# A rank for every operation, exp tile by tile in four units, and filler products in planned pauses

## The chip, the cores and the metric

The kernel runs on one core of one Trainium2 chip. The core has five instruction queues that run beside each other: TensorE (PE, matrix products; PEld is its loading of the stationary operand), VectorE (DVE), ScalarE (ACT), GpSimd (POOL) and SyncE (SP, which here only issues DMAs). Each runs its own list of instructions in order and waits on semaphores for the others. The metric is the device time of one execution in microseconds; the median of several runs counts.

## What is computed

Linear attention with random features for 8 batches of 8 heads (576 tokens, 64 channels, 128 features), and then a feed-forward layer (512 to 2048 to 512 channels, exact GELU) over the 4608 tokens:

```python
q_s, k_s = (q * scale, k * scale)
def phi(x):
    proj = np.einsum('bhsd,md->bhsm', x, omega)
    sq = np.sum(x * x, axis=-1, keepdims=True) / 2.0
    h = proj - sq
    h = h - np.max(h, axis=-1, keepdims=True)
    return np.exp(h) / np.sqrt(m)
q_p, k_p = (phi(q_s), phi(k_s))
kv = np.einsum('bhsm,bhsd->bhmd', k_p, v)
z = np.sum(k_p, axis=2)
num = np.einsum('bhsm,bhmd->bhsd', q_p, kv)
den = np.einsum('bhsm,bhm->bhs', q_p, z)[..., None] + 1e-06
x = (num / den).transpose(0, 2, 1, 3).reshape(4608, 512)
h = x @ w_in
out = (0.5 * h * (1.0 + erf(h / np.sqrt(2)))) @ w_out
```

The term sq is the same for all features of a token, so it falls out when the largest value is taken away.

## The kernel before

**Attention units.** A unit is a pair of heads of one batch; there are 32, four to a batch. Units 0 to 7 ("plain", `unit_plain`) work in float32: `pair` and `shared` project K and Q into PSUM (18 tiles of 128 tokens by 128 features), `top` on DVE takes each row's negative maximum, the exp follows, `kv` is the key-value product, `q_trans` and `q_copy` transpose the Q features, `num_plain` makes numerator and denominator, and `den`, `rcp`, `div` divide into the token buffer `xs`. The exp has two forms. In units 0 to 3 `exp_tiles` reads each tile from PSUM and takes the maximum as its bias, 18 small ACT instructions. In units 4 to 7 `shift_tiles` on DVE adds the maximum and writes to SBUF, and one ACT instruction (`exps`, 2304 columns) does the whole unit. Units 8 to 31 ("split") work with pairs of 16-bit parts: `x_high` and `x_low` split K and Q, `proj` and `proj_q` project them, `exps` is one instruction per unit, `kv_split`, `num` and `back` follow.

**Feed-forward blocks.** There are 18 blocks of 256 tokens. Block 0 runs in float32 (`mm1`, `gelu_plain`, `mm2_plain`). The others use 16-bit parts: `sw1` and `sw2` (function `product`) are the first layer in a seven-product scheme, with `comb_a`, `comb_b`, `comb_c` between them; `gelu`, `g_high` and `g_low` make the two 16-bit parts, and `mm2` is the second layer, into the PSUM buffers "acc". A block has eight chunks.

**Weights.** They come as 64-bit words in 16 pieces of two DMAs each (`w_load`, eight pieces of w_in, then eight of w_out). `w_hi` and `w_lo` (ACT), `w_shift` (DVE) and `w_round` (POOL) turn a piece into float32 in the buffer `w32`; its largest value sets a scale (`wchain_a` to `wchain_f`), and then `a_high`, `a_low`, `s_high`, `s_low` (w_in) and `w_high`, `w_low` (w_out) make the 16-bit parts. `w_high` (line 602) writes `woh`.

**What sets the order.** The program is a graph of operations, each with an engine, a cost in microseconds, and keys that it reads and writes. At build time the class `Planner` steps through a planned time: on each engine, among the operations that are ready and have room in their buffers, the one with the least due time goes next. The result is one fixed list for each engine. The due time comes from tables found outside the program (`STARTS`, `UDUE`, `OFF`, `PO`), propagated backwards through the graph, less a bonus by kind:

```python
p = (o.due - bonus.get(o.kind, 0.0), o.id)
```

PSUM has three buffers "at", three "h" and two "acc". Units of batch 0 may take any of them, units 4 to 7 only "at":

```python
ring = ANY if u.mode == 0 else 'at'
```

`put` writes an operation's instructions and ties them to the one before on the same engine.

Of the kernel before, what the change touches and what calls it, by code (L numbers as in the profile page):

```python
# [41 lines left out]
OFF = dict(a_high=-13.69, a_high2=-2.55, a_low=3.92, a_low2=30.54, back=-0.66, back_c=-53.08, block_be=18.21, block_high=2.46,  # L42
        block_high_1=-26.27, block_low=1.36, block_low_1=-19.02, block_out=1.79, block_scales=-9.32, block_spread=8.72,
        bound_a=-5.8, bound_a_a=-478.94, bound_a_b=1.62, bound_a_c=6.31, bound_b=0.18, bound_b_a=-192.28, bound_b_b=-308.58,
        bound_b_c=14.95, bound_c=-4.72, bound_c_a=85.34, bound_c_b=-108.59, bound_c_c=8.05, chain_a=-1.54, chain_b=3.92,
        chain_c=66.41, chain_d=2.96, comb_a=0.61, comb_a_1=1.25, comb_b=-1.27, comb_b_1=-14.65, comb_c=-0.14, comb_c_1=-8.99,
        den_a=-450.06, den_b=-18.7, div_a=-474.39, div_b=-35.9, exp_tiles_a=88.01, exps=3.6, exps_b=74.83, exps_c=21.55,
        g_high=-0.99, g_high_1=-58.14, g_low=-11.39, g_low_1=2.86, gelu=0.98, gelu_1=3.81, gelu_plain=-27.15, identity=-18.43,
        k_high=-2.66, k_high_c=15.22, k_low=-3.41, k_low_c=-24.51, k_shift=-2.42, k_shift_c=1.96, kv_a=-4935.28, kv_a_c=86.01,
        kv_b=-28.56, kv_b2=-1.97, kv_b2_c=14.8, kv_b_c=17.09, kv_c=7.39, kv_c_c=-27.26, kv_d=2.75, kv_d_c=12.39, kv_split=-2.52,  # L50
        kv_split_c=-3.32, kvz_plain_a=-243.1, kvz_plain_b=5.35, load_dup=-31.91, load_dup_c=179.73, load_om=15.98,
        load_two_a=-43.39, load_two_b=-51.4, load_v_a=-56.35, load_v_b=-128.76, load_vst=52.48, load_vst_c=22.44, mm1=15.82,
        mm2=25.3, mm2_1=0.3, mm2_plain=18.77, norm=-13.96, norm_c=4.14, nothing=1.34, num=-6.46, num_c=15.2, num_plain_a=-13.88,
        num_plain_b=-10.89, p2=2.99, pair_a=-272.72, pair_b=121.03, proj=0.47, proj_add=0.18, proj_add_c=-12.11, proj_c=0.24,
        proj_lo=0.22, proj_lo_c=-23.83, proj_q=0.39, proj_q_c=-12.62, put_x=-2.32, put_x_c=-12.75, q_back=2.77, q_back_c=8.16,
        q_blocks=2.07, q_blocks_c=-41.78, q_copy_a=-396.58, q_copy_b=-6.38, q_high=-0.51, q_high_c=21.5, q_low=0.22,
        q_low_c=-0.57, q_max=2.12, q_max2=0.92, q_max2_c=10.36, q_max3=13.21, q_max3_c=18.46, q_max4=-11.32, q_max4_c=7.99,
        q_max5=0.92, q_max5_c=3.49, q_max6=-15.37, q_max6_c=94.79, q_max_c=-114.63, q_shift=-18.3, q_shift_c=-152.32,
        q_trans_a=513.45, q_trans_b=-13.77, rcp_a=-364.04, rcp_b=29.11, s_high=36.92, s_low=-50.32, s_sum=-467.63,
        scale_om=-24.66, shared_a=-708.55, shared_b=-11.95, shift_tiles_b=7.13, split_om=-36.34, store=-53.19, store_dma=0.58,  # L60
        sw1=0.55, sw1_1=17.68, sw2=0.57, sw2_1=2.01, t_sum=3.22, t_sum_1=-27.4, top_a=-128.4, top_b=-0.8, v_a=4.39, v_a_c=91.42,
        v_b=0.99, v_b_c=-16.74, v_max=-14.06, v_max_c=47.43, v_scales=4.0, v_spread=32.29, vb_ones=-35.4, w_abs_1=-722.49,
        w_hi_0=1.8, w_hi_1=-202.85, w_high=-23.19, w_lo_0=3.69, w_lo_1=-90.29, w_load_0=202.81, w_load_1=4.68, w_low=-134.68,
        w_max_0=5.38, w_max_1=258.53, w_round_0=-55.99, w_round_1=-43.44, w_shift_0=8.21, w_shift_1=6.84, warm=198.7,
        wchain_a=-48.44, wchain_b=43.0, wchain_c=-25.75, wchain_d=7.44, wchain_e=16.02, wchain_f=-27.17, x_high=6.09,
        x_high_c=-14.76, x_low=-3.36, x_low_c=-0.55, zeros=37.43)
# [1452 lines left out]
```

## Time and profile before

| What | us |
|---|---|
| Median of 3 runs (969.47 to 973.82) | 972.83 |
| The profiled execution, its own time | 974.43 |
| Its span, first to last instruction | 972.4 |
| DVE, ACT, POOL busy | 762.8, 736.2, 485.1 |
| First `mm1` of block 0 | 65.15 |
| First second-layer product of block 1 | 154.59 |

In a row of the timeline stand start and length in us, engine, line, operation, what it writes and reads, how many instructions are merged, and in brackets the idle time before it and what ended that. A row of the waits gives the waiting engine and line, the one that it waited for, the sum in us, how often, and the longest. A row of windows gives a stretch, its length, and for each engine its busy time and instructions, then TensorE's granted clock as a share, the busy share of the DMA engines and GB/s. `w` is the name under which the profile shows the buffer `w32`, parts of which serve as a second feature buffer.

### The profile page before, as it was taken

To read this page: it belongs to the slowest core of one execution; us is meant where nothing else is said; L and a number is where in the kernel's file an instruction comes from. 1 tells how busy PE (TensorE), PEld (TensorE's weight loads), DVE (VectorE), ACT (ScalarE), POOL (GpSimd) and SP (SyncE) were. 2 spreads that over 40 slices of the span, in tenths; PEclk is the share of its full clock that TensorE was granted. 3 is DMA by queue.
4 is the path that set the end of the run, shared out by engine and by line. 5 is a ranking of instruction groups with operands and counts; after the bars stand their busy time and mean duration, and the time that the engine had idled before them with its cause. 6 is when DMAs were issued, how large, how long until landed. Compare 5 with 4: busy or idle time off the path is not lost.

```text
span 972.4 us, 25715 instructions
## 1 busy us (share of the span) xinstructions
PE 934.6 (96%) x9956; PEld 692.8 (71%) x9956; DVE 762.8 (78%) x2134; ACT 736.2 (76%) x1573; POOL 485.1 (50%) x717
## 2 busy tenths in 40 slices
PE   7979997889999999899999999999999999999998
PEld 6757655567776777677787777867776777786776
DVE  3878888999987998887987899788888897753432
ACT  5968868688889878877877887888787898653432
POOL 0335663775658545754638564397546764300100
PEclk7979998999999999999999999999999999999999
DMA  8865332223221313121212131212121200000000
GB/s 227 236 187 176 131 92 89 65 85 88 61 64 50 97 43 92 44 74 53 82 40 73 53 96 53 72 40 85 51 72 51 72 26 23 2 24 12 12 23 22
DMA packets 46313, 71.44 MB, mean 73 GB/s; under 512 B 13680, under 2 KB 22256, under 8 KB 46192
## 3 DMA queue, kind: packets, MB, share of 16 engines
q1 hardware_dynamic: 46192, 69.81, 23.9%
q8 instruction: 78, 1.28, 0.5%
q14 instruction: 43, 0.35, 0.1%
HBM read 60.36 MB, written 9.44 MB: 72 GB/s over the span
## 4 chain that ended last, share of the span: by engine, by line
PE 74%; DVE 9%; ACT 5%; POOL 5%; DMA 3%; issue 3%; SPq 1%; POOLq 0%; ACTq 0%; DVEq 0%
PE h L1279 26%; PE acc L1327 9%; PE acc L1328 9%; PE acc L1329 9%; PE h L1266 3%; PE acc L1320 3%; PE at L1007 2%; PE at L1092 2%; PE at L1029 2%; PE at L852 2%; PE at L797 1%; DVE w L1082 1%; DVE gl L1317 1%; DMA vt<-in_v 1%; POOL r L999 1%
## 5 line engine op out<-in xcount | busy, mean ns | idle before, releaser
L999 POOL TENSOR_TENSOR r<-xt,r 64x288 fp32r<-64x288 f32 (+2 forms) x216 | 165.9, 784 | 144.7 <-ACT r L994 83.7
L1279 PE MATMUL h<-xh,w 128*128 128x128 f16 x2176 | 216.2, 219 | 0.0
L1328 PE MATMUL acc<-woh,gl 128*128 128x512 f16 (+1 forms) x544 | 206.0, 379 | 2.5 <-DVE gl L1317 2.5
L1327 PE MATMUL acc<-woh,gh 128*128 128x512 f16 (+1 forms) x544 | 207.0, 381 | 0.9 <-ACT o L1336 0.9
L1329 PE MATMUL acc<-wol,gh 128*128 128x512 f16 (+1 forms) x544 | 205.8, 378 | 0.2 <-DVE wol L605 0.2
L1279 PE MATMUL h<-xl,w 128*128 128x128 f16 x1088 | 198.6, 219 | 0.0
L1279 PEld LDWEIGHTS <-w 128*128 128x128 f16 x3264 | 195.4, 98 | 3.3
L1279 PE MATMUL h<-xh,wih 128*128 128x128 f16 x816 | 157.2, 220 | 8.5 <-DVE gl L1317 4.8
L1279 PE MATMUL h<-xl,wih 128*128 128x128 f16 x816 | 156.5, 219 | 0.0
L1279 PE MATMUL h<-xh,wil 128*128 128x128 f16 x816 | 156.5, 219 | 0.0
L1279 PEld LDWEIGHTS <-wih 128*128 128x128 f16 x1632 | 139.7, 98 | 18.3 <-DVE h L1297 4.1
L1317 DVE SCALAR_TENSOR_TENSOR gl<-h,bs,gh 128x512 f16<-128x512 f32 x136 | 101.0, 744 | 46.2 <-ACT gh L1314 45.7
L1305 ACT ACTIVATE h<-h,bs 128x512 f32<-128x512 f32 x136 | 90.0, 662 | 49.0 <-PE h L1279 42.7
L1314 ACT ACTIVATE gh<-h,bs 128x512 f16<-128x512 f32 x136 | 93.6, 689 | 36.0 <-PE acc L1329 28.9
L1329 PEld LDWEIGHTS <-gh 128*128 128x128 f16 x560 | 55.1, 98 | 63.5 <-issue 1.7
L1279 PEld LDWEIGHTS <-wil 128*128 128x128 f16 x816 | 80.1, 98 | 17.0 <-issue 7.9
L994 ACT CAST r<-xt 128x256 fp32r<-128x256 f32 (+2 forms) x216 | 81.7, 407 | 13.2 <-PE at L1029 7.6
L1328 PEld LDWEIGHTS <-gl 128*128 128x128 f16 x560 | 55.2, 99 | 47.0 <-DVE gl L1317 3.0
L1327 PEld LDWEIGHTS <-gh 128*128 128x128 f16 x560 | 55.0, 98 | 47.2 <-issue 2.1
L1286 ACT COPY g<-h 128x256 f32<-128x256 f32 x136 | 50.4, 370 | 40.8 <-PE h L1279 38.5
L1291 DVE TENSOR_TENSOR g<-h,g 128x128 f32<-128x128 f32 x136 | 38.5, 283 | 39.0 <-ACT g L1286 38.3
L1292 DVE TENSOR_TENSOR h<-h,g 128x256 f32<-128x256 f32 x136 | 58.8, 433 | 4.7
(231 smaller groups left out, 2106.7 us busy)
## 6 DMA issues: line engine op xcount, KB each, us to landing
xt<-in_kT SPq DMA_DIRECT2D x56, 288.0 KB, 3.9
xt<-in_qT SPq DMA_DIRECT2D x56, 288.0 KB, 3.8
out_x<-o SPq DMA_DIRECT2D x35, 256.0 KB, 2.0
raw<-in_w_in SPq DMA_DIRECT2D x16, 512.0 KB, 6.6
raw<-in_w_out SPq DMA_DIRECT2D x16, 512.0 KB, 4.6
...
```

Source lines behind the costliest of these rows:

```text
L994: nc.scalar.copy(G['r', u, x][:, 0:b - a], xf[:, a:b])
L999: nc.gpsimd.tensor_tensor(r, xf[D:, a:b], r, op=ALU.subtract)
L1279: nc.tensor.matmul(h, w[p], x[r], start=first and i + m == 0, stop=last and i == 1 and m == 2, skip_group_check=True)
L1286: nc.scalar.copy(G['sa', n, c], G['h', n, c][:, 0:2 * P])
L1291: nc.vector.tensor_tensor(q, hv[:, 3], sa[:, 0:P], op=ALU.add)
L1292: nc.vector.tensor_tensor(hv[:, 1:3], hv[:, 1:3], q.unsqueeze(1).broadcast_to([P, 2, P]), op=ALU.add)
L1305: nc.scalar.activation(h, h, AF.Gelu, scale=G['bs', n][:, 2:3])
L1314: nc.scalar.activation(G['gh', n, c], G['h', n, c], AF.Copy, scale=G['bs', n][:, 3:4])
L1317: nc.vector.scalar_tensor_tensor(G['gl', n, c], G['h', n, c], G['bs', n][:, 3:4], G['gh', n, c], op0=ALU.mult, op1=ALU.subtract)
L1327: nc.tensor.matmul(acc, gh, woh[:, f, c0:c1], start=f == 0, stop=False)
L1328: nc.tensor.matmul(acc, gl, woh[:, f, c0:c1], start=False, stop=False)
L1329: nc.tensor.matmul(acc, gh, wol[:, f, c0:c1], start=False, stop=f == NF - 1)
```

## The change

**Rank.** The four tables, the backward propagation and the bonus are gone. A table `RANK` with one whole number for each operation is the due time:

```diff
-            o.due = 1e9 if k == 0 else UDUE[n] if k == 2 else add if k == 3 else add + STARTS[n] + (STARTS[n + 1] - STARTS[n] if n + 1 < len(STARTS) else 48.0) * x
-                o.due = min(o.due, s.due - o.c - (lat.get(o.e, 0) + hop.get(s.e, 0) if s.e != o.e else 0))
-            o.due += PO.get(o.id, 0.0)
-            o.due += OFF.get(o.tag, 0.0)
+            o.due = RANK[o.id]
...
-                    p = (o.due - bonus.get(o.kind, 0.0), o.id)
+                    p = o.due
...
+RANK = (0, 0, 0, 0, 1, 5, 2, 3, 8, 1, 2, 49, 4, 7, 2, 3, 5, 9, 16, 17, 13, 11, 3, 17, 38, 30, 4, 11, 13, 14, 2, 12, 19, 13, 20, 23, 25, 21, 23, 36,
```

Some 20 planned costs are changed as well (`den` from 0.5 to 0.35, `num_plain` from 1.0 to 1.15, `a_low` from 0.75 to 0.92, and others), and `proj` and `proj_q` are planned 0.057 us longer where the operation ahead of them on PE carries no mark (`psw`; the projections, `kv_split` and `back` carry one). Planned costs change the order only.

**Exp tile by tile.** The mode of units 4 to 7 becomes that of units 0 to 3, with their PSUM buffers kept to "at":

```diff
-            u.mode = 0 if b == 0 else 1 if u.k < X['plain'] else 2
+            u.mode = 0 if u.k < X['tiles'] else 1 if u.k < X['plain'] else 2
...
-        ring = ANY if u.mode == 0 else 'at'
+        ring = ANY if u.b == 0 else 'at'
```

With X['tiles'] = 8, `shift_tiles` and the whole exp are gone from units 4 to 7; each has 18 exps of one tile.

**Filler products.** Where the planner leaves PE idle by more than 0.9 us ahead of an operation that takes a new PSUM buffer, after 5 us of planned time, `put` writes products of bfloat16 views of the identity into that buffer ahead of the operation's own, whose first product starts over; nothing reads them:

```diff
+            o.idle = t - max(free[o.e], o.free) if o.e == 'PE' else 0.0
...
+        if X['fill'] and o.idle > 0.9 and o.t > 5.0:
+            t = [G[k] for (_, k), name in zip(o.new, o.pick) if name in ANY]
+            for _ in range(int((o.idle - 0.3) * X['fill'] / 0.11) if t else 0):
+                nc.tensor.matmul(t[0][:, 0:256], id16[:, 0:P], id16, start=True, stop=True)
```

The program has 22 of them: 7, 5 and 6 ahead of three of the first four projections, and 4 ahead of a later chunk of the first layer. The number of `ACT_TABLE_LOAD` instructions, which ACT needs between exp and GELU, is 60 in place of 56. `store` also names the block's scales among what it reads; that changes no instruction.

**What moves: the start.** These are the first rows of SP in the program before. `xt` holds K and Q of two units, `om` is omega, `raw` a weight piece, `vt` V.

```order
L750 DMA xt<-in_kT 128x576
L536 DMA om_66<-in_omT 64x128 x2
L750 DMA xt<-in_kT 128x576
L750 DMA xt<-in_qT 128x576 x2
L573 DMA raw<-in_w_in 128x4x256 x4
L746 DMA vt_73<-in_v 128x10x64
L746 DMA vt_74<-in_v 128x10x64
```

And the same place of SP in the changed program, where 545 is the weights' line, 722 that of K and Q:

```order
L508 DMA om_66<-in_omT 64x128 x2
L545 DMA raw<-in_w_in 128x4x256 x2
L722 DMA xt<-in_kT 128x576
L722 DMA xt<-in_qT 128x576
L722 DMA xt<-in_kT 128x576
L722 DMA xt<-in_qT 128x576
L545 DMA raw<-in_w_in 128x4x256 x2
L718 DMA vt_74<-in_v 128x10x64
```

The first weight piece now stands ahead of K and Q; V of the first two units has the same loads ahead of it as before.

**What moves: the exp of unit 4.** These are rows of ACT before, from the last weight maximum (599) to the rows behind the exp (790). Lines 578 and 583 are `w_hi` and `w_lo`, 836 is `q_copy`, 879 `den`, 816 `bound_a`.

```order
L599 ACTIVATE w_71,wmax<-w_71 128x1024
L836 COPY w_71<-h 128x512
L578 ACTIVATE raw<-raw 128x1024
L583 ACTIVATE w_71<-raw 128x1024
L879 ACTIVATE dt<-at 128x288
L790 ACTIVATE et<-et 128x2304
L836 COPY w_71<-acc 128x128
L816 ACTIVATE zr<-w_71 128x2
L578 ACTIVATE raw<-raw 128x1024
```

And rows of ACT at the same place in the changed program; 753 is the exp of tiles, 550 and 555 are `w_hi` and `w_lo`, 808 `q_copy`, 851 `den`, 571 the weight maximum:

```order
L753 ACTIVATE et<-at,nm 128x128 x4
L555 ACTIVATE w_71<-raw 128x1024
L851 ACTIVATE dt<-acc 128x288
L753 ACTIVATE et<-at,nm 128x128 x6
L808 COPY w_71<-h 128x512 x2
L550 ACTIVATE raw<-raw 128x1024
L808 COPY w_71<-at 128x128
L571 ACTIVATE w_71,wmax<-w_71 128x1024
L851 ACTIVATE dt<-acc 128x288
L788 ACTIVATE zr<-kvz 128x2
L555 ACTIVATE w_71<-raw 128x1024
L753 ACTIVATE et<-at,nm 128x128 x4
```

The one exp of unit 4 has become groups of four and six tiles with weight work between them.

**What moves: the split of the output weights.** Rows of ACT before around the twelve splits (602); 1305 and 1314 are `gelu` and `g_high` of block 1, 994 is `x_high`, 1011 `proj_lo`, 633 `s_high`:

```order
L1305 ACTIVATE h<-h,bs 128x512
L1314 ACTIVATE gh<-h,bs 128x512
L602 ACTIVATE woh<-w_71,wsc 128x512 x12
L1011 COPY lo<-at 128x256
L602 ACTIVATE woh<-w_71,wsc 128x512 x2
L633 ACTIVATE w_71<-ts,wsc 128x512
L836 COPY qh<-at 128x512
L994 CAST r<-xt 128x256
L836 COPY qh<-at 128x512
L602 ACTIVATE woh<-w_71,wsc 128x512 x2
```

And in the changed program, where 574 is the split, 605 `s_high`, 1258 `comb_a`, 1277 `gelu`:

```order
L574 ACTIVATE woh<-w_71,wsc 128x512 x9
L753 ACTIVATE et<-at,nm 128x128 x4
L808 COPY qh<-at 128x512
L605 ACTIVATE w_71<-ts,wsc 128x512 x2
L574 ACTIVATE woh<-w_71,wsc 128x512
L753 ACTIVATE et<-at,nm 128x128 x4
L574 ACTIVATE woh<-w_71,wsc 128x512 x2
L808 COPY qh<-at 128x512
L808 COPY qh<-at 128x128
L574 ACTIVATE woh<-w_71,wsc 128x512 x2
L1258 COPY g<-h 128x256
L753 ACTIVATE et<-at,nm 128x128 x2
```

Fourteen of the sixteen splits now stand ahead of the first `gelu` and `g_high` of block 1, with exps and copies between them.

More of the change, by code (lines that the diff above doesn't have):

```diff
@@ L42 @@
[L42 to L66, printed above, removed]
@@ L326, in emit @@
                 c = o.c
-                if o.tab and o.tab != self.tab:
+                if o.e == 'PE':
+                    c += X['psw'] * (o.tab == 'r' and self.ptab is None)
+                    self.ptab = o.tab
+                elif o.tab and o.tab != self.tab:
                     c += X['tsw']
@@ L349, in room @@
         def room(o):
-            t, o.pick, taken = o.ready, [], {}
+            t, o.pick, taken, o.free = o.ready, [], {}, 0.0
             if o.e == 'POOL':
@@ L373, in room @@
                 t = max(t, best[0])
+                o.free = max(o.free, best[0])
                 o.pick.append(best[1])
@@ L455, in favor_attention_ffn @@
     wi32 = w32f[:, 1].rearrange("p c (j w) -> p c j w", j=NJ)
+    id16 = ident.bitcast(BF16)
     ones = cp.tile([1, P], F32, name="ones")
@@ L921, in out_ops @@
         pn = [('pn', u, half, a) for a in range(2)]
-        ring = ANY if u.mode == 0 else 'at'
-        op('PE', 1.0, num_plain, u, half, r=[('qh', u, g) for g in (0, 1, 2)] + [('kvz', u), ('qh', u)] + old, w=keys, new=[(ring, k) for k in pn] + new)
-        op('ACT', 0.5, den, u, half, r=pn, new=[('dt', ('dt', u, half))])
+        ring = ANY if u.b == 0 else 'at'
+        op('PE', 1.15, num_plain, u, half, r=[('qh', u, g) for g in (0, 1, 2)] + [('kvz', u), ('qh', u)] + old, w=keys, new=[(ring, k) for k in pn] + new)
+        op('ACT', 0.35, den, u, half, r=pn, new=[('dt', ('dt', u, half))])
         op('DVE', 1.13, rcp, u, half, r=[('dt', u, half)], new=[('rt', ('rt', u, half)), ('rc', ('rc', u, half))])
@@ L938, in out_split @@
             keys, new, old = places(u, ps)
-            op('PE', 0.11 * n + 0.03, back, u, g, r=[('nx', u), ('nx', u, 0), ('nx', u, 1), 'ident'], new=[(('at', 'h'), ('px', u, g))])
-            op('ACT', sum(0.17 + (c1 - c0) / 1200 for _, c0, c1, _ in ps), put_x, u, g, due=(2, 2 * u.k + g, 0.0, 0.0), r=[('px', u, g)] + old, w=keys, new=new)
+            op('PE', 0.11 * n + 0.01, back, u, g, tab='q', r=[('nx', u), ('nx', u, 0), ('nx', u, 1), 'ident'], new=[(('at', 'h'), ('px', u, g))])
+            op('ACT', sum(0.06 + (c1 - c0) / 1200 for _, c0, c1, _ in ps), put_x, u, g, due=(2, 2 * u.k + g, 0.0, 0.0), r=[('px', u, g)] + old, w=keys, new=new)
     def unit_plain(u):
@@ L1207, in split_post @@
             op('POOL' if X['klp'] else 'DVE', 0.25 + 0.3 * n if X['klp'] else 0.14 + 0.15 * n, k_low, u, g, r=es, w=[('kk', g)])
-        op('PE', 0.77, kv_split, u, r=['vb'] + [('kk', g) for g in range(len(KG))], w=[], new=[('at', pk), ('kvs', ('kvs', u)), ('kvz', ('kvz', u))])
+        op('PE', 0.87, kv_split, u, tab='q', r=['vb'] + [('kk', g) for g in range(len(KG))], w=[], new=[('at', pk), ('kvs', ('kvs', u)), ('kvz', ('kvz', u))])
         op('ACT', 0.22, kv_a, u, r=[pk], w=[('kvs', u)])
@@ L1215, in split_post @@
         for g in range(2):
-            op('DVE', 0.74, q_back, u, g, r=[('eq', u.eb, y) for y in (g, g + 2)], new=[('qt', ('qt', u, g))])
+            op('DVE', 0.71, q_back, u, g, r=[('eq', u.eb, y) for y in (g, g + 2)], new=[('qt', ('qt', u, g))])
             op('ACT', 0.62, q_high, u, g, r=[('qt', u, g)] + ([('qf', u)] if g else []), w=[('qf', u, g)], new=[] if g else [('qf', ('qf', u))])
@@ L1381, in ffn_first @@
                new=[] if p else [('h', hk)], due=(1, n, (c + p * .28) / NS, 0.0), kind='P')
-        op('ACT', 0.16 + 256 / 1200, comb_a, n, c, r=[hk], new=[('g', ('sa', n, c))], kind='F')
+        op('ACT', 0.33, comb_a, n, c, r=[hk], new=[('g', ('sa', n, c))], kind='F')
         op('DVE', 0.65, comb_b, n, c, r=[('sa', n, c)], w=[hk], new=[('g', ('qs', n, c))], kind='F')
@@ L1386, in ffn_first @@
         op('ACT', 0.15 + 512 / 1000, gelu, n, c, r=[('bs', n)], w=[hk], tab='g', kind='F')
-        op('ACT', 0.7, g_high, n, c, r=[('bs', n), hk], new=[('gh', ('gh', n, c))], kind='F')
+        op('ACT', 0.66, g_high, n, c, r=[('bs', n), hk], new=[('gh', ('gh', n, c))], kind='F')
         op('DVE', 0.71, g_low, n, c, r=[('bs', n), hk, ('gh', n, c)], new=[('gl', ('gl', n, c))], kind='F')
@@ L1400, in ffn_second @@
                 if c == nc_ - 1:
-                    op('ACT', 0.68 if n else 0.6, store, n, i, c0, c1, r=[key] + ([('bo', n)] if n >= N32 else []), w=[('o', n, i)] if c0 else [],
+                    op('ACT', 0.68 if n else 0.6, store, n, i, c0, c1, r=[key] + ([('bo', n), ('bs', n)] if n >= N32 else []), w=[('o', n, i)] if c0 else [],
                        new=[] if c0 else [('o', ('o', n, i))], due=(1, n + 1, (lag + i * .6) / nc_, 0.0), kind='F' if n >= N32 else 'F0')
```

43 lines of the change are left out of this document (17 added, 26 removed), and 335 rows, old and new, of tables (PO, RANK, UDUE).

## The prediction

> **What bounds the kernel now.** I read the page first, then the busy time of each engine in five stages, then who waited for whom on TensorE (PE) in them.
>
> ```profile
> span 972.4 us, 25715 instructions
> PE 934.6 (96%) x9956; PEld 692.8 (71%) x9956; DVE 762.8 (78%) x2134; ACT 736.2 (76%) x1573; POOL 485.1 (50%) x717
> PEclk7979998999999999999999999999999999999999
> ```
>
> PE is the bound: 972.4 - 934.6 = 37.8 us are all that a better order can take out of its idle time, and the clock row (a digit for each 24.3 us) is low in the slices from 0, 49 and 146 us. What must be asked is where those 37.8 us stand. The columns of the next view are the stage, its length, and the busy time of PE, PEld, DVE, ACT and POOL.
>
> ```profile
> 0.00:62.00 62.00, 49.42 (x408) 38.90 (x408) 38.92 (x103) 45.24 (x116) 15.66 (x16) 0.84 0.77 224
> 62.00:155.00 93.00, 92.85 (x597) 64.05 (x596) 78.37 (x149) 74.67 (x115) 54.41 (x57) 1.00 0.39 131
> 155.00:210.00 55.00, 43.96 (x376) 28.82 (x375) 50.61 (x139) 43.67 (x99) 32.02 (x57) 0.91 0.25 75
> 210.00:460.00 250.00, 242.01 (x2825) 182.73 (x2824) 218.00 (x653) 204.09 (x453) 150.72 (x230) 0.99 0.24 68
> 460.00:972.40 512.40, 506.34 (x5758) 378.29 (x5757) 376.89 (x1091) 368.51 (x793) 232.32 (x359) 1.00 0.16 47
> ```
>
> PE idles 12.6 us ahead of 62, 0.2 us in 62 to 155, 11.0 us in 155 to 210, 8.0 us in 210 to 460, and 6.1 us in the last 512 us, part of which is the store after the last product. So two short stages hold 23.6 of the 37.8 us, with the low clock (0.84 and 0.91) on top. The waits in these two stages:
>
> ```profile
> PE at L797 <- ACT et L790: 5.4, 1, 5.4
> PE at L797 <- DMA vt<-in_v: 4.9, 1, 4.9
> ...
> PE at L1007 <- ACT qh L836: 2.6, 2, 2.1
> PE at L832 <- ACT qh L836: 2.6, 1, 2.6
> PE at L1092 <- DVE w L1074: 1.9, 1, 1.9
> PE h L1279 <- DVE gl L1317: 1.7, 1, 1.7
> ```
>
> The first two are single pauses: the key-value product (L797) waits for the exp of unit 4, and that of unit 0 for its V. The next two are copies out of PSUM (qh) that ScalarE (ACT) brings late.
>
> **Step 1: the exp of unit 4, tile by tile.** The rows of ACT ahead of that pause, and the product behind it beside the same product at full clock:
>
> ```profile
> 50.38 1.13 ACT L578 ACTIVATE raw<-raw 128x1024 f32<-128x1024 f32 x1 [1.74 <-DMA raw<-in_w_in]
> 51.41 1.12 ACT L583 ACTIVATE w<-raw 128x1024 int32<-128x1024 uint32 x1
> 52.73 2.11 ACT L790 ACTIVATE et<-et 128x2304 f32<-128x2304 f32 x1
> ...
> 24.62 2.26 PE L797 MATMUL at<-vt,w 128*128 128x65 f32 x18
> 54.89 4.22 PE L797 MATMUL at<-vt,et 128*128 128x65 f32 x18 [5.45 <-ACT et L790]
> ```
>
> The one exp of unit 4 stands behind two weight instructions, the first of which waits 1.74 us for its DMA; PE waits 5.45 us and then runs this product 4.22 - 2.26 = 1.96 us slower. In the new order of ACT the 18 tiles of this unit come in groups of four to six, ahead of the weight rows or between them. At most 5.45 + 1.96 = 7.4 us go; what is late next is ACT itself. Its work ahead of the copy that block 0 waits for (the denominator of unit 3, first half) comes to the same in both orders by counts, so only ACT's idle time, 62.0 - 45.2 = 16.8 us, can shrink, and of this the start keeps some (step 2). I take 6 of the 7.4 us; bounds 0 and 7.4.
>
> **Step 2: the start.** One weight piece, two DMAs, goes ahead of the first K.
>
> ```profile
> raw<-in_w_in SPq DMA_DIRECT2D x16, 512.0 KB, 6.6
> 10.00:20.00 10.00, 5.05 (x39) 4.82 (x37) 3.54 (x6) 9.22 (x33) 0.00 (x0) 0.73 1.07 302
> 7.05 1.14 ACT L781 ACTIVATE et<-at,nm 128x128 f32<-128x128 f32 x4 [5.04 <-DVE nm L777]
> 16.51 4.19 PE L797 MATMUL at<-vt,et 128*128 128x65 f32 x18 [4.95 <-DMA vt<-in_v]
> ```
>
> 1.05 MB at 302 GB/s is 3.5 us, by which the first projection, the first exp (7.05 us now) and what follows are late; all of PE's queue stands behind that projection. But V of units 0 and 1 stands behind the same bytes as before (omega, four K and Q, two weight pieces), so the product at 16.51 moves little, and ACT does 2.2 us of weight work in the time. Bounds 0 and +3.5; I take +1.
>
> **Step 3: the products without use.** 22 of them: 18 ahead of the first, third and fourth projections of the start, 4 far behind. Priced by the nearest row, that of the warm-up:
>
> ```profile
> 1.05 4.15 PE L532 MATMUL h<-w 128*128 128x256 bf16 x22 [1.05 <-DVE w L523]
> ```
>
> 4.15 / 22 = 0.19 us each, 3.4 us for the 18. The cover is the wait for the late K and Q of step 2; without it they cost those 3.4 us. None stands ahead of the first key-value product, where the 4.95 us pause and the slow 4.19 us are. So I take 0; bounds -1.9 (that product at full clock) and +3.4.
>
> The Trainium skill's page "TensorE: Matmul & The Clock Gate", section "Part 1: The HAM clock gate", says that the clock stands at half by default, rises after some 3.4 us of steady work, and falls after an idle window of that length. The trace agrees: 4.19 and 4.22 us behind pauses of about 5 us, 2.26 us in steady work. By it the fillers would help only if they left no idle window ahead of that product.
>
> **Step 4: more work for ACT.** One whole exp against 18 tiles, the table loads, and what DVE loses:
>
> ```profile
> 14.15 1.13 ACT L781 ACTIVATE w<-h,nm 128x128 f32<-128x128 f32 x4
> 15.16 1.16 ACT L781 ACTIVATE et<-h,nm 128x128 f32<-128x128 f32 x4
> L790 ACT ACT_TABLE_LOAD x27 | 34.6, 1283 | 0.5
> L786 DVE TENSOR_TENSOR et<-at,nm 128x512 f32<-128x512 f32 (+1 forms) x20 | 11.8, 628 | 0.0
> ```
>
> Four tiles take 1.01 us start to start, 18 take 4.55, so each unit costs ACT 4.55 - 2.11 = 2.4 us more, 9.8 for four. The switches between exp and gelu rise from 56 to 60, 4 x 1.28 = 5.1 us. ACT gains 14.9 us, DVE loses 11.8. In 62 to 155 ACT idles 93.0 - 74.7 = 18.3 us while PE idles 0.2: this hides it. These units may use only the three "at" buffers of PSUM, and a tile now holds one until ACT's exp has read it, not DVE's shift, so a late exp stops PE too. If the cover is gone, it costs up to 14.9 us. The nearest row is that of 62 to 155, so I take 0.
>
> The Trainium skill's page "ScalarE: Activation LUTs", section "What ACT_TABLE_LOAD costs", adds a drain of about 1.38 us to the load, 2.66 us for a switch, which speaks against this change. The measured group differs: 27 loads of 1.283 us with 0.5 us of idle time before all of them. By the page the four switches would be 10.6 us, by the row 5.1.
>
> **Step 5: the late copies at 155 to 210.**
>
> ```profile
> 0.00:149.63 149.63, 114.54 (x223) 0.93 0.56 174
> ...
> 149.63 0.69 ACT L1314 ACTIVATE gh<-h,bs 128x512 f16<-128x512 f32 x1
> 150.21 7.47 ACT L602 ACTIVATE woh<-w,wsc 128x512 f16<-128x512 f32 x12
> 159.68 0.57 ACT L836 COPY qh<-at 128x512 f32<-128x512 f32 x1
> ...
> 154.59 0.38 PE L1327 MATMUL acc<-woh,gh 128*128 128x512 f16 x1
> 160.31 0.33 PE L832 MATMUL at<-ident,et 128*128 128x128 f32 x1 [2.58 <-ACT qh L836]
> ```
>
> ACT splits the output weights in one run of twelve, with the copy of the transposed Q behind it, and PE waits. In the new order 14 of the 16 splits stand ahead of the first g_high, broken up by exps and copies. The waits for qh (5.2 us) and the slow clock behind them should go. What is late next is that first g_high: ACT has ahead of it 64 more tiles (64 x 0.2525 = 16.2 us) instead of four exps (8.4), 14 splits (14 x 0.62 = 8.7), two more loads (2.6), and ten smaller instructions less (about 4): 114.5 + 15.1 = 129.6 us of work. With step 1 taken it must start near 145, so ACT may idle 15 us ahead of it, against 149.6 - 114.5 = 35.1 now. The start keeps about 12 of these. It is tight but can be met, since 18.3 of the 35.1 stand where PE was the bound. I take -5 us; bounds 0 and -11.0.
>
> **Step 6: the rest.** Of the 8.0 us idle in 210 to 460 I take 2 (bounds 0 and 8.0), as DVE, which ends the g_low that PE waits for, has 11.8 us less to do. Behind 460, where PE is full, a new order can only lose: +1 (bounds 0 and +4, the idle time there is 6.1 us now).
>
> **Sum.** -6 + 1 + 0 + 0 - 5 - 2 + 1 = -11 us. The profiled execution took 974.43 us, 2.0 more than its span, and lies 1.6 over the median of 972.83. So 963.4 for such an execution and **962 us** for the median.
>
> **Rivals.** First, **slower: ACT becomes the bound.** For it: 15.1 us more work ahead of the first g_high than now. If ACT keeps its 35.1 us of idle time there, that g_high starts at 164.7 and with it the first second-layer product of block 1; the 14 splits done by then (8.7 us) are given back behind it, net +6.4, 979 us. It decides when ACT idles more than 35.1 - 15.1 = 20 us ahead of it. Against it: the 0.2 us of PE's idle time in 62 to 155.
>
> Second, **no change: the gain waits at the output weights.** The weight conversions stand about as deep in ACT's order as before, so if DMA and their rounding set the pace, PE reaches the second-layer product early and waits until about 154.6; only steps 5 and 6 in small part remain, 970 us. For it: the 1.74 us wait for a weight DMA; against: the queue starts the first piece ahead of K now.
>
> Third, **the fillers do what they are meant for** and the first key-value product runs at full clock: 1.9 us more, 960 us. Against it: none stands ahead of it. If they do nothing, the forecast stands.
>
> Fourth, **much more goes**: steps 1, 5 and 6 to their ends (7.4 + 11.0 + 8.0 - 1), 974.4 - 25.4 - 1.6 = 947 us.
>
> **How the numbers follow.** Chances: forecast (955 to 968) 0.45, third 0.05, fourth (943 to 955) 0.15, no change 0.19, slower 0.16. A difference under 0.5%, 4.9 us, can't be told from none here. Faster: 0.45 + 0.05 + 0.15, less 0.02 for the upper edge of the forecast, 0.63; same 0.20; slower 0.17. The range 946 to 978 leaves out the far half of the fourth and most of the slower one.
>
> **What would show it.** Step 1: no wait of PE over 2 us at the key-value product of unit 4, and the mean clock in 50 to 62 at 0.9 or more. Step 2: the first projection at about 8 us instead of 5. Step 4: ACT busy near 751 us, DVE near 751. Step 5: the first second-layer product (its matmul on woh and gh) at 145 to 151 us, and no wait for qh over 1 us. Step 6: PE idle under 7 us behind 460. A start of that product after 155 us would make the forecast wrong by the slower rival; a wait of PE for the output weights at it, by the second.

## The result, and the profile after

The changed kernel takes 946.70 us (median of four, 945.67 to 947.03), the kernel before 972.64 us in runs beside it. The ratio is 0.9737, with a 95% interval of 0.9712 to 0.9761: 26 us less, where 11 were forecast. The profiled execution took 946.9 us, and its page begins so:

```profile
span 945.1 us, 25838 instructions
PE 926.2 (98%) x9978; PEld 688.2 (73%) x9978; DVE 747.6 (79%) x2114; ACT 747.0 (79%) x1645; POOL 492.2 (52%) x717
PEclk9999999999999999999999999999999999999999
```

PE's idle time fell from 37.8 to 945.1 - 926.2 = 18.9 us, and its busy time by 8.4 us although 22 products were added: the low slices of the clock row are gone. The same five stages as before (stage, length, busy time of PE, PEld, DVE, ACT and POOL with their instructions, granted clock, DMA share, GB/s):

```profile
0.00:62.00 62.00, 54.52 (x462) 40.77 (x464) 40.58 (x110) 51.54 (x140) 18.04 (x18) 0.97 0.84 248
62.00:155.00 93.00, 91.39 (x591) 60.47 (x588) 78.91 (x141) 87.45 (x174) 47.50 (x51) 1.00 0.40 131
155.00:210.00 55.00, 53.62 (x575) 39.88 (x572) 51.54 (x150) 47.46 (x107) 41.91 (x67) 1.00 0.23 71
210.00:460.00 250.00, 245.98 (x2849) 186.02 (x2849) 220.16 (x674) 212.58 (x470) 161.85 (x241) 1.00 0.24 70
460.00:945.10 485.10, 480.73 (x5513) 361.07 (x5511) 356.41 (x1044) 348.00 (x758) 222.92 (x343) 1.00 0.16 46
```

What PE loses in a stage has two parts: its idle time, and what the low clock costs while it works, about (1 - clock) times its busy time. The first stage is cut at 25 us below, by the same view of both kernels: PE was busy 18.20 of 25 us at a clock of 0.80 and 31.22 of 37 us at 0.87, and is now busy 21.44 at 1.00 and 33.09 at 0.95.

| Stage, us | Lost before: idle + clock | Lost after | Change | Forecast |
|---|---|---|---|---|
| 0 to 25 | 6.8 + 3.6 | 3.6 | -6.8 | +1 (steps 2, 3) |
| 25 to 62 | 5.8 + 4.1 | 3.9 + 1.7 | -4.3 | -6 (step 1) |
| 62 to 155 | 0.2 | 1.6 | +1.4 | 0 (step 4) |
| 155 to 210 | 11.0 + 4.0 | 1.4 | -13.6 | -5 (step 5) |
| 210 to 460 | 8.0 + 2.4 | 4.0 | -6.4 | -2 (step 6) |
| 460 to the end | 6.1 | 4.4 | -1.7 | +1 (step 6) |

The sum is -31.4. The fillers add 22 x 0.13 = 2.9 us of work (five of them take 0.65 us), so -28.5; the spans differ by 27.3. The rest can be the clock column, which has two digits (0.01 of it is 2.4 us in the fourth row). The first row holds 18 of the fillers as work, about 2.3 us, and it differs between executions: e9 below, the same program once more, loses 4.7 us there, and e1, without fillers, 7.9. The loss of 155 to 210 us is the largest single change. Its waits now, all of them:

```profile
PE h L1251 <- DVE gl L1289: 0.8, 1, 0.8
PE h L1251 <- DVE xl L1233: 0.6, 1, 0.6
```

The rows that the forecast named as its signs, from the timeline of PE and of ACT and a window that ends at the first g_high:

```profile
8.47 1.16 PE L737 MATMUL at<-om,xt 64*128 64x128 f32 x16 [1.16 <-DMA xt<-in_kT]
...
15.87 1.21 PE L769 MATMUL at<-vt,w 128*128 128x65 f32 x8 [0.38 <-ACT w L753]
...
52.79 2.28 PE L769 MATMUL at<-vt,et 128*128 128x65 f32 x18
...
145.91 0.38 PE L1299 MATMUL acc<-woh,gh 128*128 128x512 f16 x1 [0.41 <-ACT o L1306]
```

```profile
128.53 5.62 ACT L574 ACTIVATE woh<-w,wsc 128x512 f16<-128x512 f32 x9 [1.02 <-POOL wsc L631]
...
144.69 0.69 ACT L1286 ACTIVATE gh<-h,bs 128x512 f16<-128x512 f32 x1
```

```profile
0.00:144.65 144.65, 136.16 (x965) 95.59 (x967) 109.41 (x227) 128.76 (x289) 64.05 (x65) 0.99 0.56 173
```

The key-value product of unit 4 (52.79) has no wait and full clock, that of the first unit (15.87) waits 0.38 us instead of 4.95, and the first second-layer product of block 1 comes at 145.91 instead of 154.59. ACT did 128.76 us of work ahead of the first g_high and idled 15.9. In the whole kernel ACT is busy 747.0 us and DVE 747.6, where about 751 was forecast for each.

### The profile page after: what moved, and what is told of

The parts are those of the page before. It is cut to its first block, busy times and chain, and to the rows that moved or that the text cites. A ratio compares the mean times of both kernels' runs of the same rounds, so it can differ in the third digit from the quotient of the medians.

```text
span 945.1 us, 25838 instructions
## 1 busy us (share of the span) xinstructions
PE 926.2 (98%) x9978; PEld 688.2 (73%) x9978; DVE 747.6 (79%) x2114; ACT 747.0 (79%) x1645; POOL 492.2 (52%) x717
## 4 chain that ended last, share of the span: by engine, by line
PE 75%; ACT 9%; DVE 8%; POOL 6%; issue 2%; DMA 1%; SPq 0%; POOLq 0%; ACTq 0%; DVEq 0%
PE h L1251 28%; PE acc L1299 10%; PE acc L1300 10%; PE acc L1301 10%; PE h L1238 3%; PE at L1001 2%; PE at L979 2%; PE at L824 2%; PE at L1064 2%; PE acc L1292 2%; POOL ts L1220 2%; ACT et L753 1%; ACT woh L574 1%; POOL r L971 1%; ACT w L753 1%
## 5 line engine op out<-in xcount | busy, mean ns | idle before, releaser
L971 POOL TENSOR_TENSOR r<-xt,r 64x256 fp32r<-64x256 f32 (+2 forms) x216 | 168.6, 796 | 113.3 <-ACT r L966 92.0
L1251 PE MATMUL h<-xh,w 128*128 128x128 f16 x2176 | 218.2, 219 | 0.0
L1251 PE MATMUL h<-xl,w 128*128 128x128 f16 x1088 | 199.3, 219 | 0.6 <-DVE xl L1233 0.6
L1251 PEld LDWEIGHTS <-w 128*128 128x128 f16 x3264 | 195.8, 98 | 4.9 <-issue 0.7
L1251 PE MATMUL h<-xh,wih 128*128 128x128 f16 x816 | 156.9, 220 | 4.0 <-DVE h L1269 1.9
L1251 PE MATMUL h<-xl,wih 128*128 128x128 f16 x816 | 156.1, 219 | 0.3 <-DVE xl L1233 0.3
L1251 PE MATMUL h<-xh,wil 128*128 128x128 f16 x816 | 156.2, 219 | 0.0
L1251 PEld LDWEIGHTS <-wih 128*128 128x128 f16 x1632 | 139.4, 98 | 19.3 <-DVE h L1269 3.4
L966 ACT CAST r<-xt 128x256 fp32r<-128x256 f32 (+2 forms) x216 | 84.1, 407 | 14.4 <-PE at L979 5.5
L1251 PEld LDWEIGHTS <-wil 128*128 128x128 f16 x816 | 80.0, 98 | 11.2 <-issue 2.1
L1258 ACT COPY g<-h 128x256 f32<-128x256 f32 x136 | 50.5, 371 | 34.5 <-PE h L1251 33.8
L1263 DVE TENSOR_TENSOR g<-h,g 128x128 f32<-128x128 f32 x136 | 38.3, 282 | 28.5 <-ACT g L1258 27.7
```

The costliest lines, as they stand in the source:

```text
L966: nc.scalar.copy(G['r', u, x][:, 0:b - a], xf[:, a:b])
L971: nc.gpsimd.tensor_tensor(r, xf[D:, a:b], r, op=ALU.subtract)
L1251: nc.tensor.matmul(h, w[p], x[r], start=first and i + m == 0, stop=last and i == 1 and m == 2, skip_group_check=True)
L1258: nc.scalar.copy(G['sa', n, c], G['h', n, c][:, 0:2 * P])
L1263: nc.vector.tensor_tensor(q, hv[:, 3], sa[:, 0:P], op=ALU.add)
```

## The experiments

To try a part of the new order alone, most of these kernels replace the choice among ready operations by a list of operation numbers:

```diff
-            o.due = RANK[o.id]
...
+        for i in ORDER:
+            o = self.ops[i]
+            t = room(o)
+            emit(o, max(t, free[o.e]))
```

OLD is the list that the kernel before issues, NEW that of the changed kernel, each with the planned time of every operation. `upto(OLD, 62)` stands for what OLD has issued by 62 us, `rest(NEW)` for all else in NEW's order. `tiles` puts the exps of units 4 to 7 where the shifts stood and drops the whole exps; `whole` does the reverse. Fillers are kept where the first part of the list is NEW. In e5, e8, e13 and e14 an operation whose inputs come later in the list is held until they are issued.

The last two columns are PE's loss (idle + clock, as above) by the profile of each run; before it is 0.2 and 15.0 us, after 1.6 and 1.4.

| Run | Order, exps of units 4 to 7 | us, median | Ratio to before, 95% | 62 to 155 | 155 to 210 |
|---|---|---|---|---|---|
| e1 | NEW, no fillers | 947.78 | 0.9753 (0.9726 to 0.9780) | 1.5 | 1.4 |
| e2 | tiles(OLD) | 982.08 | 1.0107 (1.0073 to 1.0141) | 11.4 | 12.6 |
| e3 | OLD to 62, then NEW; tiles | 955.14 | 0.9826 (0.9797 to 0.9856) | 5.3 | 1.6 |
| e4 | NEW to 60, then OLD; tiles | 982.12 | 1.0106 (1.0076 to 1.0136) | 13.4 | 13.8 |
| e5 | whole(NEW) | 959.52 | 0.9861 (0.9843 to 0.9879) | 4.8 | 4.6 |
| e6 | NEW, splits of w_out late | 956.86 | 0.9831 (0.9811 to 0.9850) | 12.6 | 3.0 |
| e7 | NEW, gelus of block 0 twice | 948.54 | 0.9750 (0.9731 to 0.9769) | 3.0 | 1.4 |
| e8 | NEW to 60, then OLD; whole | 986.36 | 1.0139 (1.0121 to 1.0157) | 14.7 | 11.3 |
| e9 | NEW, as it is | 947.04 | 0.9744 (0.9722 to 0.9765) | 1.5 | 1.4 |
| e10 | NEW, no fillers | 948.14 | 0.9753 (0.9731 to 0.9776) | 1.5 | 1.4 |
| e11 | NEW, more fillers | 947.49 | 0.9749 (0.9726 to 0.9772) | 1.5 | 1.4 |
| e12 | NEW to 145, then OLD; tiles | 973.21 | 1.0011 (0.9997 to 1.0024) | 6.8 | 13.8 |
| e13 | NEW, unit 8 early | 972.89 | 0.9992 (0.9980 to 1.0003) | 8.9 | 13.1 |
| e14 | OLD, unit 8 late; whole | 1000.17 | 1.0273 (1.0253 to 1.0293) | 0.1 | 21.0 |
| e15 | OLD to 140, then NEW; tiles | 973.01 | 0.9995 (0.9982 to 1.0008) | 11.4 | 12.7 |
| e16 | OLD to 205, then NEW; tiles | 979.00 | 1.0061 (1.0040 to 1.0081) | 11.4 | 13.5 |
| e17 | NEW, 3.2 us more on DVE | 948.71 | 0.9768 (0.9749 to 0.9788) | 1.5 | 2.7 |
| e18 | OLD, 3.2 us more on DVE; whole | 974.20 | 1.0027 (1.0013 to 1.0042) | 0.2 | 15.5 |

### Fillers: e1, e9, e10, e11

```diff
-X = dict(pm=0.15, tsw=1.28, psw=0.057, plain=8, tiles=8, fill=0.6, kvp=8, eb0=8, ttr=1,
+X = dict(pm=0.15, tsw=1.28, psw=0.057, plain=8, tiles=8, fill=0, kvp=8, eb0=8, ttr=1,
```

That is e1 and e10. In e11 the list names the fillers by operation (9 is the first projection, 99 a transpose of unit 2's Q):

```diff
-FILL = {9: 7, 17: 5, 52: 6, 1338: 4}
+FILL = {9: 16, 17: 5, 52: 6, 1338: 4, 99: 11}
```

> The changed kernel without its 22 products without use; every other instruction keeps its place on every engine. Theory A (the order carries the gain, the fillers are only covered by the wait for the later K and Q): 944 to 948 us, the first key-value product still takes about 2.3 us and no half-clock stretch comes before 30 us. Theory B (the fillers keep the clock up at the start): the first key-value product takes over 3.5 us, the clock falls somewhere in 10 to 30 us, and the time is 950 to 954 us, some 4 to 7 us more, as the two half-clock stretches ahead of 62 us cost the kernel before 7.7 us. Theory C (the fillers cost PE time that nothing hides): 943.5 us, 22 x 0.15 us less.

> The changed kernel once more, beside the next two on the same chip, so that differences of 0.1 to 0.3% can be told: 946 to 948 us. Its own spread from execution to execution is that of the arrival of the first K: PE waited 1.16 us for it in the profiled one, up to 3.1 us in kernels with the same first instructions.

> The changed kernel without its fillers, beside it. By the traces the fillers ahead of the first projection lie in the wait for K and keep the clock up: 2.95 us less half-clock loss in 7.9 to 14.8 us; the 11 others there cost 1.33 us in the open. Theory B' (they pay by that difference): 1 to 2 us more than the changed kernel. Theory K (the 1.1 us seen lies in the noise): within 0.5 us of it.

> The changed kernel with 16 fillers instead of 7 ahead of the first projection (9 x 0.11 us, of which 1.16 us are idle now), and 11 new ones in the 1.69 us wait at 39.8 us, behind which the clock is at half from 41.2 to 44.6 us. Theory B' (a filled wait keeps the clock up): that half-clock stretch goes, 1.7 us less, 945 to 946 us. Theory K: no change, or the stretch only moves to a later place, as it did without fillers, where it stood at 55.7 us: 946.5 to 948 us.

Without fillers the first projection and the first key-value product look like this on PE (e1):

```profile
8.59 2.08 PE L737 MATMUL at<-om,xt 64*128 64x128 f32 x16 [3.29 <-DMA xt<-in_kT]
...
16.69 2.35 PE L769 MATMUL at<-vt,w 128*128 128x65 f32 x18
```

K comes at about the same time, but the projection takes 2.08 us instead of 1.16, at half clock; the fillers had turned 3.29 us of idle time into 1.16. They don't always keep the clock up: in e9, with the same fillers, the first projection takes 1.16 us too, but PE runs at 0.50 from 10.0 to 13.4 us. The key-value product has full clock without them too. Where the half clock falls, by windows of e1, of the changed kernel and of e11 (two):

```profile
8.00:14.50 6.50, 5.91 (x48) 5.03 (x48) 3.00 (x5) 5.94 (x13) 2.35 (x1) 0.50 1.12 336
```

```profile
41.20:44.60 3.40, 3.40 (x28) 2.36 (x26) 2.75 (x7) 3.09 (x6) 0.80 (x1) 0.50 1.01 317
```

```profile
18.40:25.00 6.60, 6.60 (x31) 6.33 (x31) 1.93 (x6) 6.38 (x19) 0.58 (x1) 0.50 0.86 253
41.20:44.60 3.40, 3.40 (x40) 2.64 (x39) 2.54 (x8) 2.85 (x8) 1.32 (x1) 1.00 0.94 292
```

In both pairs (e1 against the result, e10 against e9) the fillers are worth 1.1 us, less than the width of the ratios' intervals: theory B' has the size right, B is refuted (4 to 7 us), and nothing is left of C. Theory A has the time of e1, but not its sign, since PE runs at half clock from 8.0 to 14.5 us. In e11, with the wait at 39.8 us filled too, no half-clock stretch stands behind it, but one stands at 18.4 us: no gain, as theory K said. That the filling moved it is not shown, since e1 and e10, one and the same program, have their second stretch at 55.8 and at 41.4 us.

### The exp tile by tile, in the old order and in the new: e2, e5

```
e2: ORDER = tiles(OLD)
e5: ORDER = whole(NEW)
```

> The kernel before with its own order on every engine, in which only the exp of units 4 to 7 is done tile by tile (the tiles stand where DVE's shifts stood, the whole exps go); no fillers. Theory A (the order carries the gain): the 5.45 us wait of PE at unit 4's key-value product goes, the waits in 155 to 210 us stay; 966 to 973 us. Theory D (the exps tile by tile carry the gain, since DVE loses 11.8 us and the long exps go): 958 us or less. Theory E (in an order not made for it ACT's 14.9 us more work comes out): 975 to 985 us.

> The changed kernel in its new order, but with the exps of units 4 to 7 whole, as before (DVE's shifts where the tiles stood, one exp behind the last of them; what needs an exp not yet issued comes behind it). Theory A (the new order is made of the tiles, a key-value product stands close behind the last K tile): PE waits for the whole exps again, 952 to 962 us. Theory H (the place of the work counts, not the form of the exp): 944 to 949 us, since ACT has 9.7 us less work and 4 table loads less. The tiles alone, in the old order, cost 10 us.

The waits of PE in 62 to 155 us of e2, and in 50 to 62 us of e5:

```profile
PE at L814 <- ACT et L753: 6.1, 2, 4.4
PE at L737 <- ACT et L753: 1.7, 1, 1.7
```

```profile
PE at L769 <- ACT et L762: 5.7, 1, 5.7
```

In the old order the tiles cost 982.1 - 971.9 = 10.2 us (971.93 is the kernel before in the runs beside it). ACT comes too late for `num_plain` (L814) and a projection's buffer (L737): this is the forecast's slower rival, in the order where it holds. In the new order the tiles are worth 959.5 - 946.7 = 12.8 us: with whole exps the wait at unit 4's key-value product is back, 5.7 us. So E holds for e2 and A for e5; A and D fall for e2, H for e5. The same edit has opposite signs in the two orders.

### The start: e3, e4, e8

```
e3: ORDER = upto(tiles(OLD), 62) + rest(NEW)
e4: ORDER = upto(NEW, 60) + rest(tiles(OLD))
e8: ORDER = upto(NEW, 60) + rest(OLD), exps whole in both parts
```

> The operations that the kernel before issues in about its first 62 us, in its order, then all others in the order of the changed kernel; exps tile by tile throughout, no fillers at the start. Theory A (the losses of PE are separate by stage: 20.3 us ahead of 62 us before, 9.2 after, 3 of the difference being fillers): 953 to 958 us, with a start like that of the kernel before and under 3 us of PE idle in 155 to 210 us. Theory F (one chain: the weights that the changed order brings 15 to 20 us earlier in the first 60 us are what removes the loss behind 155 us): 962 to 972 us, with over 8 us of PE idle in 150 to 215 us.

> The operations that the changed kernel issues in about its first 60 us, in its order, fillers too, then all others in the order of the kernel before; exps tile by tile throughout. Theory A: only the start is gained, 963 to 967 us, and the loss behind 155 us (15.1 us) stays. Theory F (the early weights remove the later loss as well, whatever order follows): 950 to 956 us. Theory G (what the start gains waits later for the order of before): 970 to 974 us.

> The operations that the changed kernel issues in about its first 60 us, in its order, all others in the order of the kernel before, and the exps of units 4 to 7 whole throughout. The same with tiles took 982 us, no less than the tiles alone in the order of before. Theory A (the start is worth its 8 us where the old order does not have to carry the tiles): 963 to 967 us. Theory G (what the start gains waits later in the old order): 970 to 974 us.

Under the new order the new start is worth 955.1 - 946.7 = 8.4 us, the fillers' 1.1 among them (theory A). Under the old order it is worth nothing (e4 against e2) or less than nothing (e8, 13 us above the kernel before). All expectations for e4 and e8 missed: those for e4 left out the 10 us that the tiles cost in the old order, and those for e8 did not have the old order lose more than it does with its own start. The stage behind the start, 62 to 155 us, in e3, e4 and e8:

```profile
62.00:155.00 93.00, 89.51 (x548) 60.09 (x545) 73.29 (x131) 82.80 (x157) 48.53 (x49) 0.98 0.34 114
```

```profile
62.00:155.00 93.00, 82.91 (x456) 54.02 (x454) 59.09 (x111) 76.03 (x150) 43.52 (x47) 0.96 0.34 114
```

```profile
62.00:155.00 93.00, 86.01 (x475) 59.43 (x476) 64.57 (x123) 61.34 (x93) 40.78 (x42) 0.91 0.36 117
```

PE is busy 82.91 and 86.01 of 93 us there in e4 and e8, at a clock of 0.96 and 0.91: what was gained ahead is lost again behind.

### The splits of the output weights: e6

In rows of ACT, the changed kernel against e6 (574 is `w_high`, 1286 g_high, 1306 the store of block 0):

```diff
-L574 ACTIVATE woh<-w_71,wsc 128x512 x9
 L753 ACTIVATE et<-at,nm 128x128 x4
 L808 COPY qh<-at 128x512
...
 L1277 ACTIVATE h<-h,bs 128x512
 L1286 ACTIVATE gh<-h,bs 128x512
+L574 ACTIVATE woh<-w_71,wsc 128x512 x14
 L1306 COPY o<-acc 128x512
```

> The changed kernel with one thing moved: the 14 splits of the output weights that stood ahead of the first g_high on ACT (and their second halves on DVE) stand right behind it, in one run. All else keeps its place. Theory A (the place of this run against the first g_high and the copies behind it is what cost 15 us of PE time in 155 to 210 us): a wait of PE of over 3 us at the second-layer products of block 1 or at the copies behind the run, 955 to 962 us. Theory I (the run can be hidden; DVE and the attention work moved out of 155 to 210 us made the difference): 946 to 950 us.

The run of splits on ACT, and the second-layer product of block 1 on PE:

```profile
145.08 8.67 ACT L574 ACTIVATE woh<-w,wsc 128x512 f16<-128x512 f32 x14
153.65 0.57 ACT L1306 COPY o<-acc 128x512 f32<-128x512 f32 x1
```

```profile
154.27 0.59 PE L1299 MATMUL acc<-woh,gh 128*128 128x512 f16 x1 [9.09 <-ACT o L1306]
```

Theory A: PE waits 9.09 us for the copy behind the run, and runs at half clock after it (0.59 us a product, not 0.38); 10.2 us in all. The early place of the splits is needed in the new order. The loss stands elsewhere than before, in 62 to 155 us (12.6) and not in 155 to 210 (3.0); both stages together lose 15.6 us, 15.2 in the kernel before and 3.0 in the changed one.

### Room on ACT and on DVE: e7, e17, e18

```diff
-        nc.scalar.activation(g_plain(c), G['h', 0, c][:, 0:TB[0]], AF.Gelu)
+        nc.scalar.activation(g_plain(c), G['h', 0, c][:, 0:TB[0]], AF.Gelu); nc.scalar.activation(g_plain(c), G['h', 0, c][:, 0:TB[0]], AF.Gelu)
```

```diff
-        nc.vector.tensor_reduce(vmax[:, u.k:u.k + 1], u.v[:, :, 0:D], axis=AX.XY, op=ALU.max, apply_absolute_value=True)
+        for _ in range(2 if u.b == 2 else 1): nc.vector.tensor_reduce(vmax[:, u.k:u.k + 1], u.v[:, :, 0:D], axis=AX.XY, op=ALU.max, apply_absolute_value=True)
```

> The changed kernel with each of the 16 gelus of block 0 done twice (the same values again): 16 x 0.25 to 0.38 us, 4 to 6 us more of ACT's work in 62 to 120 us. It measures how much room ACT has ahead of the first g_high, where it idles 144.65 - 128.76 = 15.9 us, some 10 of them in the first 62 us. Theory A (ACT is as tight as the forecast's slower rival said): the first g_high 3 to 6 us later and 949 to 953 us. Theory J (ACT has room): 946 to 948 us.

> The changed kernel with the maxima over V of units 8 to 11 taken twice on DVE (the same values again), 4 x 0.81 = 3.2 us more of DVE's work at 154 to 165 us, where DVE idles 3.7 us in 60. Theory Q (DVE sets the pace there now): 949 to 951 us, 2 to 4 us more than the changed kernel. Theory R (DVE has room behind PE's queue): 946 to 948 us. The same test of ACT, 6 us more in 62 to 120 us, gave 1.8 us.

> The kernel before with the same 3.2 us more on DVE, which stand at 186 to 195 us there. Theory Q' (DVE is what PE's waits at 190 to 205 us hang on in the old order too): 974 to 977 us. Theory R': 971 to 974 us, no change beyond 0.5%.

By the profiles ACT did 5.0 us more ahead of the first g_high in e7, which came at 145.9 us instead of 144.7; the kernel took 1.8 us more. 3.2 us more on DVE in 154 to 165 us cost 2.0 (948.71 - 946.70). These runs were not made beside the changed kernel; by the ratios the costs are 1.3 and 3.0 us, each less than the width of the intervals (0.4%, 3.8 us). Both lie between the theories: as far as these runs can tell, neither engine has room for all of it, and neither passes all of it on. In the old order the same DVE work costs 2.6 us, with an interval of 0.1 to 0.4%.

### The order behind 145 us: e12 to e16

```
e12: ORDER = upto(NEW, 145) + rest(tiles(OLD))
e13: ORDER = NEW, operations of unit 8 planned behind 140 us issued as if 20 us earlier
e14: ORDER = OLD, operations of unit 8 planned behind 140 us issued as if 15 us later
e15: ORDER = upto(tiles(OLD), 140) + rest(NEW)
e16: ORDER = upto(tiles(OLD), 205) + rest(NEW)
```

> The operations that the changed kernel issues in about its first 145 us, in its order, fillers too, all others in the order of the kernel before; exps tile by tile. The 14 early splits of the output weights are among the first. Theory A (the splits ahead of the first g_high are what 155 to 210 us needed): PE loses under 5 us in 155 to 210 us (15.1 before, 1.4 in the changed kernel), and what the order behind 210 us brings is missing: 950 to 956 us. Theory L (the order of DVE and PE behind 145 us counts as much): 8 us and more lost in 155 to 210 us, 956 to 964 us.

> The changed kernel with the operations of unit 8 (the first split unit) that it issues behind about 140 us moved some 20 us ahead in every engine's order, where their inputs allow it: its key-value product then has 294 feed-forward products of the first and 72 of the second layer ahead of it, as in the kernel before (318 and 72), not 468 and 102. All else keeps its order. Theory M (before, PE stood at unit 8's products too early, with feed-forward work that was ready queued behind them): 4 to 10 us more, 951 to 957 us, with a wait at that key-value product. Theory N (the place of unit 8 does not matter by itself): 946 to 949 us.

> The kernel before, whole exps and its own order, with the operations of unit 8 behind about 140 us moved some 15 us back in every engine's order: 444 and 96 feed-forward products ahead of its key-value product. Theory M: the waits at that product (1.95 us) and ahead of it shrink, 965 to 970 us. Theory N: 972 to 976 us, the waits for the copy of the transposed Q (5.2 us) behind the late splits stay, or unit 8 now comes too late for what follows it.

> The operations that the kernel before issues in about its first 140 us, in its order, all others in the order of the changed kernel; exps tile by tile, no fillers at the start. With the old order throughout and tiles: 982 us, of which PE loses 28.7 us ahead of 155 us, 12.2 in 155 to 210 us, 16 behind. Theory A' (the order behind 140 us is what keeps PE fed there, whatever came ahead): under 4 us lost in 155 to 215 us and 962 to 968 us. Theory O (it needs the early weights): over 8 us lost there and 970 to 978 us.

> The operations that the kernel before issues in about its first 205 us, in its order, all others in the order of the changed kernel; exps tile by tile. Theory A' (the 7 us gained behind 210 us are that order's own): 974 to 977 us. Theory P (they follow from what came ahead, for example from how far DVE is behind): 980 to 983 us.

The stage 155 to 210 us of e12, e13 and e15:

```profile
155.00:210.00 55.00, 46.77 (x390) 32.60 (x391) 46.23 (x134) 39.64 (x92) 35.92 (x62) 0.88 0.26 80
```

```profile
155.00:210.00 55.00, 43.17 (x388) 27.89 (x387) 41.29 (x114) 37.43 (x85) 31.51 (x55) 0.97 0.23 75
```

```profile
155.00:210.00 55.00, 46.44 (x415) 31.20 (x414) 44.84 (x120) 38.33 (x86) 27.64 (x54) 0.91 0.21 68
```

In e12 the order ahead of 145 us is that of the changed kernel, the splits too, and the first g_high comes at 145.10 us (144.69 there); still PE loses 13.8 us here: 26 us of gain become none, more than theory L allowed. In e15 the new order behind 140 us finds the old state ahead of it, and loses 12.7 us, most in one wait (theory O). Neither part brings it alone; e3, with the old order to 62 us only, loses 1.6, although its first g_high comes as late as 152.6 us. The waits of e13 in 145 to 210 us and of e15 in 155 to 210 us:

```profile
PE h L1251 <- DVE h L1269: 9.8, 4, 5.2
PE acc L1300 <- DVE vexp L1103: 3.8, 1, 3.8
```

```profile
PE h L1251 <- DVE h L1269: 8.6, 1, 8.6
```

In both, the first layer's products (L1251) wait for the addition `comb_c` on DVE (L1269). DVE is busy 41.29 and 44.84 of 55 us there, so it is not full: the addition needs the copy `comb_a` (L1258), and ACT brings that late. The rows of ACT in e13 and in e15:

```profile
145.44 1.02 ACT L966 CAST r<-xt 128x256 fp32r<-128x256 f32 x3 [3.65 <-DMA xt<-in_kT]
...
146.98 0.35 ACT L1258 COPY g<-h 128x256 f32<-128x256 f32 x1
```

```profile
158.91 8.68 ACT L574 ACTIVATE woh<-w,wsc 128x512 f16<-128x512 f32 x14 [1.53 <-POOL wsc L631]
167.50 0.35 ACT L1258 COPY g<-h 128x256 f32<-128x256 f32 x1
```

In e13 ACT stands at the split of unit 8's K (L966) for 3.65 us until that K has landed. Its load is issued at 140.6 us, 139.7 in the changed kernel: the operations of unit 8 were moved ahead and the load was not. In e15 the copy stands behind a run of 14 splits of the output weights, the same cause as in e6.

The move of unit 8 costs 26 us in e13 instead of the 4 to 10 of theory M, and in the old order its move to later costs 26.5 us (e14), so all theories for both runs missed. That it is unit 8's place which matters so much is not shown: part of e13's cost is the load that was left behind, and no other unit was moved by as much. e16 gains 982.1 - 979.0 = 3.1 us on e2 (4.5 by the ratios), so of the 8 us won behind 210 us about half are that order's own, between theories A' and P.

No run was faster than the changed kernel; of these, only e11 was tried in the hope of it.

## Why the prediction was wrong

The pauses named in steps 1 and 5 went. What failed is the size of the terms of steps 5 and 6, and the sign of step 2. Against the forecast, step 5 took 8.6 us more out, step 6 7.1, and steps 2 and 3 about 5.5, the fillers' own work aside; steps 1 and 4 took 3.1 less. The fourth rival (much more goes, a chance of 0.15) has the direction, but that its 947 us is the measured time is in good part luck: its terms for steps 1, 5 and 6 were 7.4, 11.0 and 8.0 with 1 us lost at the start, and the stages gave 4.3, 13.6 and 8.1 with about 4.5 us gained at the start.

**Step 1** was right: no wait at unit 4's key-value product, and full clock there; the stage shows -4.3 for the -6 forecast, since a new wait (1.69 us at 39.8 us) and a half-clock stretch came in. That the wait goes because of the tiles is shown by e5.

**Step 2** was forecast as a cost of 1 us and stands in a stage that gained 6.8, about 4.5 without the fillers' own work. The first projection comes at 8.47 us, as forecast, but the later K moves PE's work into the wait for V: the first key-value product starts at 15.87 us (16.51 before; 16.69 in e1, 17.34 in e9), and in none of the three is there a wait for V. Its pause of 4.95 us is gone, and it runs at full clock, without fillers too. The prediction said that this product "moves little", and did not ask what then becomes of the pause ahead of it. Which of the moves at the start does it was not tried one by one; e3 gives their sum, 8.4 us.

**Step 3** took 0; measured are 1.1 us gained. The third rival's sign came (the product at full clock), but e1 shows it without fillers.

**Step 4** took 0 for ACT's 14.9 us, and that held for the new order: 128.76 us of work ahead of the first g_high (129.6 forecast), 15.9 us idle (15 allowed), g_high at 144.69 (145). But this is no term by itself, as the prediction had it: the same tiles cost 10.2 us in the old order and save 12.8 in the new.

**Step 5** is the term most at fault: -5 with bounds 0 and -11.0, against -13.6. The bounds held the idle time alone. The clock of 0.91 in the same row costs 0.09 x 43.96 = 4.0 us more. Step 5 named the slow clock but gave it no price, as step 1 had done for its own pause. And of the 11.0 us the prediction counted the 5.2 us of waits for qh, the only ones for which it had named a cause; the others (1.9 and 1.7 us for DVE in the row of waits, and smaller ones) went too. The cause named, the late run of splits, is borne out by e6 and e15: such a run makes PE wait for 9.09 and 8.6 us. It is not the whole cause: in e12 the splits stand early, and the loss is 13.8 us.

**Step 6** took -2 and +1 against -6.4 and -1.7, and its reason, less work for DVE, falls: in e5 DVE has the shifts of units 4 to 7 again, and the stage 210 to 460 us loses the same, as this row of e5 shows (4.25 us idle, 4.02 in the changed kernel):

```profile
210.00:460.00 250.00, 245.75 (x2830) 185.99 (x2828) 221.30 (x682) 212.03 (x476) 162.49 (x238) 1.00 0.25 72
```

By e16 about half of this gain is the new order's own. Where the rest comes from stays open.

**The sum.** Each term was taken within its bounds as if it could come or not by itself. e4, e12 and e15 show that the terms hang together: with one part of the order exchanged, gains are lost whole, in e15 also in a stage that has the new order. Such a mixed order has a seam, at which neither order was planned for what it finds, and a part of these losses may be the seam's own; in e3 it costs little. That ACT meets the first g_high by 145 us decides nothing by itself: e12 meets it and takes 973.2 us, e3 is at 152.6 and takes 955.1. What stays open is what in the order behind 145 us keeps PE fed, and on which engine; no run changed the order of one engine alone there.
